# A float64-to-float32 weight conversion: the sign byte moves from VectorE to GpSimd, one buffer and a 32-byte pad are added

## The chip, the cores and the metric

One core of a Trainium2 chip runs the whole program. The metric is the device time of one execution in microseconds, the median of several runs. Engines are called PE (TensorE's matmuls), PEld (its weight loads), DVE (VectorE), ACT (ScalarE), POOL (GpSimd) and SP (SyncE, which only issues transfers here).

## What is computed

```python
attn = softmax(mask(q @ k.T / sqrt(64))) @ v          # 4 batches, 8 heads, 576 tokens, head size 64
x    = heads side by side                             # 2304 tokens x 512
x    = ((x @ w_a) * (x @ w_b)) @ w_out                # 512 -> 1536 -> 512
h    = x @ w_in;  out = (h * sigmoid(h)) @ w_out2     # 512 -> 2048 -> 512
```

Heads 0 to 3 see the last 32 keys, heads 4 to 7 every 32nd key. The weights come as float64, 8 bytes each; the activations are float32.

## The kernel before

**Stages.** The tokens are five groups of 512 (the last has 256). Attention of batch 0 stands ahead of all; the batches 1 to 3 are worked in between the first feed-forward work, by a plan. Then come 136 blocks for the groups 0 and 1: per block 12 matmuls of 128x512 with one weight piece of 128x512 (2.72 us of PE). Groups 2 and 3 follow together, by a scheme of seven products in place of eight (`Chain` from line 1005, `twin` from 1087): its products take sums of activations as moving operands, one after the other `A11, A12, S2, S1, S3, A22, S4`, in that order of `CHAIN_ORDER`, 12 matmuls each for a pair of chains (a "twin"). There are ten twins: six in the first feed-forward, four in the second, there with pieces of three other matmuls between halves of six. `A11`, `A12` and `S3` lie in tiles of `xpool`; `S2`, `S1`, `A22` and `S4` in the tile `operands` of the pool `late` (`open_late`). Group 4 comes partly between, partly last.

**Weights.** A float32 product is made of two rounded parts, so each weight piece is split: ACT writes the rounded part (L728), DVE the rest (L729, `split_w`), and the 12 matmuls of a block wait for both. Ahead of that, 68 pieces are converted from float64 once, by steps over the two 32-bit words of each number:
- `load_words` (L659, L661, on SP's queue) brings 512 KB into one of five buffers `words`, four blocks before the conversion (phase A).
- `rebase_w` (step B, L685, ACT) scales the high word into `e`.
- `merge_w` step 0 (L702, ACT) makes the three bits that come from the low word's top byte, as a whole 32-bit word of `raw`. Step 1 (L705, DVE) writes the sign bit over that word's top byte. Step 2 (L708, DVE) shifts `e` left and ors the word in.
- `keep_w` (L721) stores the piece to DRAM through POOL's queue, one block later, for the later token groups. `load_raw` (L675, SP) brings kept pieces back.

The first six pieces (`EARLY`) are converted during the attention of batch 0, where POOL does step 0 (L698); the other 62, which the change is about, in blocks 3 to 91. `raw` tiles take turns in the five buffers of `rpool`, `words` in the five of `kpool`.

**What sets the order.** Each engine runs its instructions in the order in which `block` writes them. That order is a string per phase:

```python
STEPS = ("NRM0BK1O2YXW", "N0O1B2MKWYRX")    # phase A, phase B
```

N is the softmax's guard, reciprocal and POOL product (L511, L518, L524), M its mask and maximum (L473, L484), X its exponentials (L499), O the store of attention results (L623, L626), R transposes of q and k (L288), K `keep_w`, Y `split_w`, W the loads. An instruction that waits holds back all that stand behind it on its engine.

**Memory.** Pools on the left are laid one after the other from below (`rpool`, then `wpool`, `spool`, `kpool`, `epool` behind it); `lpool`, `qpool`, `apool` are laid from the top downwards, and later `late` takes their place. In the built program every tile on the left but the narrow softmax ones starts at a multiple of 64 bytes within a partition, and the tile `operands` at byte 167904, which is 32 past one.

Of the kernel before, what the change touches and what calls it, by code (L numbers as in the profile page):

```python
# [9 lines left out]
F32 = mybir.dt.float32  # L10
F32R = mybir.dt.float32r
BF16 = mybir.dt.bfloat16
I32 = mybir.dt.int32
U8 = mybir.dt.uint8
AF = mybir.ActivationFunctionType
# [98 lines left out]
def attention_gated_mlp_silu_mlp(  # L114
# [35 lines left out]
    xpool = ctx.enter_context(tc.tile_pool(name="xpool", bufs=1))  # L150
    hpool = ctx.enter_context(tc.tile_pool(name="hpool", bufs=4))
    tpool = ctx.enter_context(tc.tile_pool(name="tpool", bufs=2))
    rpool = ctx.enter_context(tc.tile_pool(name="rpool", bufs=5))
    wpool = ctx.enter_context(tc.tile_pool(name="wpool", bufs=5))
    spool = ctx.enter_context(tc.tile_pool(name="spool", bufs=4))
    kpool = ctx.enter_context(tc.tile_pool(name="kpool", bufs=5))
# [3 lines left out]
    ringp = ctx.enter_context(tc.tile_pool(name="ringp", bufs=2, space=bass.MemoryType.PSUM))  # L160
    attp = ctx.enter_context(tc.tile_pool(name="attp", bufs=2, space=bass.MemoryType.PSUM))

    att_ctx = ExitStack()
    lpool = att_ctx.enter_context(tc.tile_pool(name="lpool", bufs=1, side="right"))
    qpool = att_ctx.enter_context(tc.tile_pool(name="qpool", bufs=2, side="right"))
# [520 lines left out]

    made = {}

    def merge_w(c, step, early=False):
        if c is None or (c < EARLY and not early):  # L690
            return
        high = words[c].bitcast(U8).rearrange("p (n eight) -> p n eight", eight=8)[:, :, 7]
        if step == 0:
            made[c] = rpool.tile([P, DM], F32, tag="raw", name="raw")
            z = made[c].bitcast(I32)
            top = words[c].bitcast(U8).rearrange("p (n eight) -> p n eight", eight=8)[:, :, 3]
            if early:
                nc.gpsimd.tensor_scalar(  # L698
                    out=z, in0=top, scalar1=1.0 / 32, scalar2=-31.0 / 64, op0=ALU.mult, op1=ALU.add
                )  # L700
            else:
                nc.scalar.activation(out=z, in_=top, func=AF.Copy, scale=1.0 / 32, bias=-31.0 / 64)  # L702
        elif step == 1:
            out = made[c].bitcast(U8).rearrange("p (n four) -> p n four", four=4)[:, :, 3]
            nc.vector.tensor_single_scalar(out=out, in_=high, scalar=SIGN, op=ALU.bitwise_and)  # L705
        else:
            z = made[c].bitcast(I32)
            nc.vector.scalar_tensor_tensor(  # L708
                out=z, in0=rebased.pop(c), scalar=3, in1=z, op0=ALU.logical_shift_left, op1=ALU.bitwise_or
            )  # L710
            del words[c]
            if c < NA:
                raw[c] = made[c]

    def keep_w(c):

        if c in made:
            kept[pieces[c]] = t = dpool.tile([P, DM], F32, tag="kept%s%d" % pieces[c], name="kept%s%d" % pieces[c])

            queue = nc.sync if c < EARLY else nc.gpsimd  # L720
            queue.dma_start(out=t, in_=made.pop(c))  # L721
# [74 lines left out]
    def block(p):  # L796


        background(p, "load")
        w = split.pop(p)  # L800
        yield w
        c = conv_at.get(p)
        for step in STEPS[p >= NA]:
            if step == "K":
                keep_w(conv_at.get(p - 1))
            elif step == "B":
                rebase_w(c)
            elif step in "012":
                merge_w(c, int(step))
            elif step == "Y":  # L810
                split_w(p + AHEAD_SPLIT)
            elif step == "W":
                load_words(conv_at.get(p + AHEAD_WORDS - AHEAD_MERGE))
                load_raw(p + (7 if p < last_conv + 2 else 9))
            else:
                background(p, {"M": "mask", "O": "store", "X": "softmax", "N": "normalise", "R": "prepare"}[step])
        background(p + 1, "tensor", "turned")
        yield None
# [680 lines left out]
```

## Time and profile before

| | us |
|---|---|
| three runs | 924.67, 928.13, 928.27 (median 928.13) |
| the profiled execution | 925.8 |
| its span, first to last instruction | 924.0 |
| PE, PEld busy | 901.9 (98%), 733.5 (79%) |
| DVE, ACT, POOL busy | 642.6 (70%), 533.3 (58%), 92.8 (10%) |
| mean granted clock of PE | 0.988 |

The profile gives each engine's busy time; a matmul's end is modelled, so one that starts late shows in the distance between starts rather than in its length. The blocks 0 to 135 lie in about 56 to 474 us of the span (the attention of batch 0 fills what is ahead), the twins of the first feed-forward in 474 to 614, those of the second in 706 to 823, group 4 between and behind them. Lines are those of the kernel before.

### The profile page before, as it was taken

The numbers are of one execution on the slowest core, as the hardware profiler recorded it, in microseconds if no ns is written. First come the engines' busy times: TensorE is split into PE (matmuls) and PEld (weight loads), VectorE is DVE, ScalarE is ACT, GpSimd is POOL, SyncE is SP. The second block draws the span as 40 slices with busy tenths as digits, with TensorE's granted clock in tenths as the row PEclk, the third lists the DMA queues.
The fourth block names the chain that finished last, engine by engine and source line by source line (L and its number), as shares of the span: only waits on it lengthen the run. The fifth ranks groups of instructions, "written<-read, shape, count | busy, mean of one in ns | idle before, by whom it ended". The sixth has DMA issues, their size and how long they took to land.

```text
span 924.0 us, 16415 instructions
## 1 busy us (share of the span) xinstructions
PE 901.9 (98%) x5907; PEld 733.5 (79%) x5914; DVE 642.6 (70%) x1215; ACT 533.3 (58%) x1270; POOL 92.8 (10%) x162
## 2 busy tenths in 40 slices
PE   8899899999999999999999999999999999999998
PEld 5577677787778878778888888888999878878897
DVE  3577888776767867666677676655687766766475
ACT  4657788665677665564544344355575655554474
POOL 4532222011111010100000000000000000000000
PEclk9699999999999999999999999999999999999999
DMA  9999899999799992323332112233463121225471
GB/s 163 191 295 252 291 267 277 274 245 271 220 261 257 290 279 87 126 80 96 104 112 76 53 55 66 68 103 103 136 183 115 47 91 57 81 81 170 123 205 39
DMA packets 163697, 145.32 MB, mean 157 GB/s; under 512 B 96848, under 2 KB 119952, under 8 KB 163616
## 3 DMA queue, kind: packets, MB, share of 16 engines
q1 hardware_dynamic: 154758, 121.81, 49.6%
q0 software_dynamic: 6912, 21.66, 7.1%
q10 hardware_dynamic: 1946, 0.81, 0.4%
q8 instruction: 46, 0.75, 0.3%
q14 instruction: 35, 0.29, 0.1%
HBM read 121.70 MB, written 22.54 MB: 156 GB/s over the span
## 4 chain that ended last, share of the span: by engine, by line
PE 71%; DVE 9%; ACT 7%; DMA 7%; issue 4%; SPq 2%; POOL 0%; DVEq 0%; ACTq 0%; POOLq 0%
PE ring L736 16%; PE ring L1022 12%; PE att L1022 9%; PE acc L1083 8%; PE acc L1437 6%; PE acc L1209 4%; PE ring L1083 4%; PE att L1083 4%; PE acc L736 3%; PE acc L1417 3%; ACT prs L499 2%; DVE w L729 2%; DMA words<-in_moe_w_b_dram 1%; DMA keptb<-raw 1%; DVE raw L708 1%
## 5 line engine op out<-in xcount | busy, mean ns | idle before, releaser
L736 PE MATMUL ring<-x,w 128*128 128x512 f32 (+1 forms) x816 | 166.4, 356 | 4.8 <-DVE w L729 3.3
L736 PEld LDWEIGHTS ring<-x,w 128*128 128x128 f32 x816 | 132.2, 189 | 30.7 <-DVE w L729 7.6
L1313 DVE TENSOR_TENSOR w<-raw,w 128x512 fp32r<-128x512 f32 (+1 forms) x164 | 106.2, 655 | 29.3 <-ACT w L1312 26.5
L1312 ACT CAST w<-raw 128x512 fp32r<-128x512 f32 (+1 forms) x164 | 95.7, 592 | 20.8 <-PE att L1083 11.0
L729 DVE TENSOR_TENSOR w<-raw,w 128x512 fp32r<-128x512 f32 x136 | 93.4, 693 | 4.9 <-ACT w L728 4.7
L1437 PE MATMUL acc<-w,h 128*128 128x512 f32 x384 | 93.7, 393 | 1.3 <-DVE w L729 0.9
L736 PE MATMUL ring<-y,w 128*128 128x512 f32 x384 | 93.6, 393 | 0.3 <-DVE w L729 0.3
L1437 PEld LDWEIGHTS acc<-w,h 128*128 128x128 f32 x384 | 71.3, 188 | 18.1 <-DVE w L729 2.1
L736 PEld LDWEIGHTS ring<-y,w 128*128 128x128 f32 x384 | 71.3, 188 | 15.9 <-DVE w L729 0.7
L728 ACT CAST w<-raw 128x512 fp32r<-128x512 f32 x136 | 82.5, 619 | 2.2 <-PE acc L736 1.3
L1417 PE MATMUL acc<-h,w 128*128 128x512 f32 x288 | 72.3, 397 | 3.6 <-DVE w L729 2.5
L746 ACT CAST h<-h 128x512 fp32r<-128x512 f32 (+1 forms) x48 | 27.2, 567 | 83.8 <-DVE h L1058 41.0
L1417 PEld LDWEIGHTS acc<-h,w 128*128 128x128 f32 x288 | 52.8, 188 | 17.8 <-DVE w L729 4.6
L1022 PE MATMUL ring<-operands,w 128*128 128x512 f32 x240 | 61.3, 398 | 0.0
L1022 PE MATMUL att<-operands,w 128*128 128x512 f32 x240 | 60.4, 396 | 0.0
L747 DVE TENSOR_TENSOR h<-g,h 128x512 fp32r<-128x512 f32 (+1 forms) x64 | 39.9, 624 | 28.9 <-ACT h L746 28.9
L1022 PE MATMUL ring<-x,w 128*128 128x512 f32 x240 | 59.4, 391 | 0.0
L746 ACT CAST h<-g 128x512 fp32r<-128x512 f32 (+1 forms) x64 | 36.3, 567 | 37.5 <-DVE g L1409 30.5
L1128 POOL DMA_DIRECT2D out_dram<-o x16 | 8.7, 545 | 467.4 <-DVE o L1127 467.0
L499 ACT ACTIVATE prs<-sm,nm 128x54 f32<-128x54 f32 (+1 forms) x120 | 39.8, 333 | 25.1 <-DVE nm L484 25.1
L1022 PEld LDWEIGHTS ring<-operands,w 128*128 128x128 f32 x240 | 44.9, 188 | 11.7 <-DVE w L1313 1.1
L1022 PEld LDWEIGHTS att<-operands,w 128*128 128x128 f32 x240 | 45.1, 188 | 10.9
(202 smaller groups left out, 1559.4 us busy)
## 6 DMA issues: line engine op xcount, KB each, us to landing
raw<-keptp SPq DMA_DIRECT2D x80, 256.0 KB
raw<-kepti SPq DMA_DIRECT2D x64, 256.0 KB
words<-in_moe_w_out_dram SPq DMA_DIRECT2D x28, 512.0 KB
raw<-kepto SPq DMA_DIRECT2D x48, 256.0 KB
raw<-kepta SPq DMA_DIRECT2D x36, 256.0 KB
raw<-keptb SPq DMA_DIRECT2D x36, 256.0 KB
words<-in_moe_w_in_dram SPq DMA_DIRECT2D x16, 512.0 KB
words<-in_moe_w_a_dram SPq DMA_DIRECT2D x12, 512.0 KB
```

The source lines that it names most:

```text
L499: nc.scalar.activation(out=place[s], in_=src[s], func=AF.Exp, bias=st["nm"][:, s:s + 1], scale=1.0, accum_out=su[:, s:s + 1],)
L728: nc.scalar.copy(out=o[:, 0], in_=t)
L729: nc.vector.tensor_tensor(out=o[:, 1], in0=t, in1=o[:, 0].bitcast(F32), op=ALU.subtract)
L736: nc.tensor.matmul(ps[:, :T], lhsT=w[:, wi, c * P:(c + 1) * P], rhs=x[:, xi, c, :T], start=(c == 0 and wi == 0 and xi == 0), stop=(c == CC ...
L746: nc.scalar.copy(out=o[:, 0, :T], in_=t32[:, :T])
L747: nc.vector.tensor_tensor(out=o[:, 1, :T], in0=t32[:, :T], in1=o[:, 0, :T].bitcast(F32), op=ALU.subtract)
L1022: nc.tensor.matmul(self.acc[acc], lhsT=w[:, wi, (2 * part + c) * P:(2 * part + c + 1) * P], rhs=x[:, xi, c], start=(begin and c == 0 and m ...
L1083: nc.tensor.matmul(accs[d], lhsT=lhsT, rhs=rhs, start=(first and wi == 0 and xi == 0), stop=(last and wi == 1))
L1312: nc.scalar.copy(out=o[:, 0, cols], in_=t)
L1313: nc.vector.tensor_tensor(out=o[:, 1, cols], in0=t, in1=o[:, 0, cols].bitcast(F32), op=ALU.subtract)
L1417: nc.tensor.matmul(accs[d], lhsT=w[:, wi, d * P:(d + 1) * P], rhs=h[:, xi], start=(j == 0 and wi == 0 and xi == 0), stop=(j == N1 - 1 and ...
L1437: nc.tensor.matmul(accs[t][:, :DM], lhsT=h[:, xi, t * P:(t + 1) * P], rhs=w[:, wi, :], start=(j == 0 and wi == 0 and xi == 0), stop=(j == ...
```

## The change

For the 62 later pieces the sign is made by POOL one block ahead: it allocates the `raw` tile and writes a whole word, -2^31 or 0 (`sign_w`, called at step 1 with the piece of block p+1). ACT's step 0 then writes only the lowest byte of each word of that tile. DVE's step 1 is gone for them; step 2 is as before. Since a tile is taken one block sooner, `rpool` has six buffers, which moves the pools behind it up by 2048 bytes; a pad of 32 bytes at the top of the right side moves all tiles there down by 32 bytes, `operands` to byte 167872, a multiple of 64. Other tiles move likewise: `qT`, `kT`, `vl`, `qld`, `kld` from 32 past a multiple of 64 onto one; `vs`, `prs`, `ptl`, `pt` and the masks from a multiple to 32 past one.

```diff
-    rpool = ctx.enter_context(tc.tile_pool(name="rpool", bufs=5))
+    rpool = ctx.enter_context(tc.tile_pool(name="rpool", bufs=6))
...
+    ppool = ctx.enter_context(tc.tile_pool(name="ppool", bufs=1, side="right"))
+    ppool.tile([P, 8], F32, name="pad")
...
+    def bytes_of(t, size, at):
+        return t.bitcast(U8).rearrange("p (n size) -> p n size", size=size)[:, :, at]
+
+    def sign_w(c):
+        if c is None or c < EARLY:
+            return
+        made[c] = rpool.tile([P, DM], F32, tag="raw", name="raw")
+        nc.gpsimd.tensor_scalar(
+            out=made[c].bitcast(I32), in0=bytes_of(words[c], 8, 7), scalar1=float(SIGN), scalar2=-(2.0 ** 31),
+            op0=ALU.is_ge, op1=ALU.mult,
+        )
...
             else:
-                nc.scalar.activation(out=z, in_=top, func=AF.Copy, scale=1.0 / 32, bias=-31.0 / 64)
+                nc.scalar.activation(
+                    out=bytes_of(made[c], 4, 0), in_=top, func=AF.Copy, scale=1.0 / 32, bias=-31.0 / 64
+                )
...
-            elif step in "012":
+            elif step in "02":
                 merge_w(c, int(step))
+            elif step == "1":
+                sign_w(conv_at.get(p + 1))
```

On POOL, in phase A during the attention of batch 1 (L721, now L738, stores a converted piece; L524, now L526, is the softmax's product; L700 is the new sign). Before:

```order
L524 TENSOR_TENSOR prs_111<-prs_111,rs 128x256
L721 DMA keptb_1469<-raw 128x512
L524 TENSOR_TENSOR prs_109<-prs_109,rs 128x256
L721 DMA kepto_1511<-raw 128x512
L524 TENSOR_TENSOR prs_110<-prs_110,rs 128x128
```

Now:

```order
L526 TENSOR_TENSOR prs_115<-prs_115,rs 128x256
L738 DMA keptb_1474<-raw 128x512
L700 TENSOR_SCALAR raw<-words 128x512
L526 TENSOR_TENSOR prs_113<-prs_113,rs 128x256
L738 DMA kepto_1516<-raw 128x512
L700 TENSOR_SCALAR raw<-words 128x512
L526 TENSOR_TENSOR prs_114<-prs_114,rs 128x128
```

The sign for block p+1 stands behind the softmax product of block p and the store of the piece of block p-1, and ahead of the softmax product of block p+1.

On DVE at the same place (L705 the sign byte, L708 the merge, now L725; L729 the split, now L746). Before:

```order
L288 STREAM_TRANSPOSE kT<-kld 128x18x32
L705 TENSOR_SCALAR raw<-words 128x512
L708 SCALAR_TENSOR_TENSOR raw<-e,raw 128x512
L729 TENSOR_TENSOR w<-raw,w 128x512
L288 STREAM_TRANSPOSE kT<-kld 128x18x32
L705 TENSOR_SCALAR raw<-words 128x512
L708 SCALAR_TENSOR_TENSOR raw<-e,raw 128x512
L729 TENSOR_TENSOR w<-raw,w 128x512
```

Now:

```order
L290 STREAM_TRANSPOSE kT<-kld 128x18x32
L725 SCALAR_TENSOR_TENSOR raw<-e,raw 128x512
L746 TENSOR_TENSOR w<-raw,w 128x512
L290 STREAM_TRANSPOSE kT<-kld 128x18x32
L725 SCALAR_TENSOR_TENSOR raw<-e,raw 128x512
L746 TENSOR_TENSOR w<-raw,w 128x512
```

The sign's row is gone and nothing else has changed places; ACT has the same rows in the same order.

## Rows read from the trace of the kernel before

**Rows 1.** Busy time by stretch: us, then busy us of PE, PEld, DVE, ACT, POOL
```profile
56.00:130.00 74.00, 69.70 (x604) 53.28 (x603) 59.91 (x121) 54.47 (x144) 16.91 (x29) 1.00 0.98 270
130.00:345.00 215.00, 210.67 (x1656) 167.74 (x1655) 159.16 (x302) 150.50 (x381) 33.41 (x59) 1.00 1.00 264
...
474.00:656.00 182.00, 182.00 (x794) 148.70 (x793) 119.01 (x206) 80.58 (x149) 2.20 (x4) 1.00 0.26 80
...
706.00:833.00 127.00, 126.74 (x552) 102.05 (x551) 90.81 (x162) 69.43 (x132) 0.00 (x0) 1.00 0.24 73
```

**Rows 2.** Timeline of PE, 97 to 112 us; in brackets the idle time before
```profile
99.18 2.56 PE L736 MATMUL ring<-x,w 128*128 128x512 f32 x10 [1.24 <-DVE w L729]
...
111.30 0.97 PE L736 MATMUL ring<-x,w 128*128 128x512 f32 x3 [1.21 <-DVE w L729]
```

**Rows 3.** Timeline of DVE, 108 to 112 us
```profile
108.30 1.25 DVE L288 STREAM_TRANSPOSE kT<-kld 128x576 f32<-128x576 f32 x1
109.39 0.45 DVE L705 TENSOR_SCALAR raw<-words 128x512 uint8<-128x512 uint8 x1
...
111.16 1.25 DVE L288 STREAM_TRANSPOSE kT<-kld 128x576 f32<-128x576 f32 x1
```

**Rows 4.** Chain that ended last, pieces in order: start us, us, what
```profile
84.18 7.20 DMA words<-in_moe_w_b_dram
...
101.23 0.46 DVE raw L705
...
318.77 0.40 DVE raw L705
```

**Rows 5.** Groups by line: count, busy us, mean ns, idle time before them
```profile
L728 ACT CAST w<-raw 128x512 fp32r<-128x512 f32 x136 | 82.5, 619 | 2.2 <-PE acc L736 1.3 <-DVE raw L708 0.9
...
L702 ACT ACTIVATE raw<-words 128x512 int32<-128x512 uint8 x62 | 41.5, 670 | 10.0 <-DMA words<-in_moe_w_a_dram 2.0 <-DMA kepto<-raw 2.0 <-issue 1.7
...
L705 DVE TENSOR_SCALAR raw<-words 128x512 uint8<-128x512 uint8 x68 | 32.1, 472 | 16.3 <-ACT raw L702 12.0 <-POOL raw L698 3.9
```

**Rows 6.** Timeline of POOL, two stretches
```profile
24.29 0.65 POOL L698 TENSOR_SCALAR raw<-words 128x512 int32<-128x512 uint8 x1
...
131.30 0.92 POOL L524 TENSOR_TENSOR prs<-prs,rs 128x324 f32<-128x324 f32 x1 [2.33 <-ACT raw L702]
132.17 0.57 POOL L721 DMA_DIRECT2D kepto<-raw  x1
```

**Rows 7.** Timeline of DVE, 131 to 135 us
```profile
131.78 0.99 DVE L708 SCALAR_TENSOR_TENSOR raw<-e,raw 128x512 int32<-128x512 int32 x1
...
133.98 0.69 DVE L708 SCALAR_TENSOR_TENSOR raw<-e,raw 128x512 int32<-128x512 int32 x1
```

**Rows 8.** Timeline of ACT, 132 to 134 us
```profile
132.62 0.67 ACT L702 ACTIVATE raw<-words 128x512 int32<-128x512 uint8 x1
```

**Rows 9.** Chain that ended last, first feed-forward's twins: start us, us, what
```profile
476.65 2.72 PE att L1022 x12
479.37 2.81 PE ring L1022 x12
482.18 2.80 PE att L1022 x12
...
493.36 2.76 PE ring L1022 x12
```

**Rows 10.** Timeline of PE in the second feed-forward's twins
```profile
755.26 0.86 PE L1083 MATMUL acc<-w,h 128*128 128x512 f32 x3
755.96 1.56 PE L1022 MATMUL ring<-operands,w 128*128 128x512 f32 x6
757.36 0.86 PE L1083 MATMUL acc<-w,h 128*128 128x512 f32 x3
```

**Rows 11.** Chain that ended last, two pieces of attention matmuls: start us, us, what
```profile
213.85 1.31 PE att L458 x80
...
237.56 1.30 PE att L593 x80
```

More of the change, by code (lines that the diff above doesn't have):

```diff
@@ L691, in merge_w @@
             return
-        high = words[c].bitcast(U8).rearrange("p (n eight) -> p n eight", eight=8)[:, :, 7]
         if step == 0:
-            made[c] = rpool.tile([P, DM], F32, tag="raw", name="raw")
-            z = made[c].bitcast(I32)
-            top = words[c].bitcast(U8).rearrange("p (n eight) -> p n eight", eight=8)[:, :, 3]
+            top = bytes_of(words[c], 8, 3)
             if early:
+                made[c] = rpool.tile([P, DM], F32, tag="raw", name="raw")
                 nc.gpsimd.tensor_scalar(
-                    out=z, in0=top, scalar1=1.0 / 32, scalar2=-31.0 / 64, op0=ALU.mult, op1=ALU.add
+                    out=made[c].bitcast(I32), in0=top, scalar1=1.0 / 32, scalar2=-31.0 / 64, op0=ALU.mult, op1=ALU.add
                 )
             else:
-                nc.scalar.activation(out=z, in_=top, func=AF.Copy, scale=1.0 / 32, bias=-31.0 / 64)
+                nc.scalar.activation(
+                    out=bytes_of(made[c], 4, 0), in_=top, func=AF.Copy, scale=1.0 / 32, bias=-31.0 / 64
+                )
         elif step == 1:
-            out = made[c].bitcast(U8).rearrange("p (n four) -> p n four", four=4)[:, :, 3]
-            nc.vector.tensor_single_scalar(out=out, in_=high, scalar=SIGN, op=ALU.bitwise_and)
+            nc.vector.tensor_single_scalar(
+                out=bytes_of(made[c], 4, 3), in_=bytes_of(words[c], 8, 7), scalar=SIGN, op=ALU.bitwise_and
+            )
         else:
@@ L715, in keep_w @@
     def keep_w(c):
-        if c in made:
+        if c is not None and c in made:
             kept[pieces[c]] = t = dpool.tile([P, DM], F32, tag="kept%s%d" % pieces[c], name="kept%s%d" % pieces[c])
```

## The prediction

> **What bounds the kernel now.** I read the busy time by stretch first. In the twins of both feed-forwards PE is busy without a gap: 182.00 of 182 us and 126.74 of 127 [rows 1]. DVE and ACT have room there, so whatever shortens a matmul shortens the kernel, and nothing else does. In 56 to 345 us, where the 62 pieces are converted, PE is idle for 74 - 69.70 = 4.3 us and 215 - 210.67 = 4.3 us [rows 1], 8.6 us together. That is small, but DVE is busy 60 of 74 us in the first of these stretches, and what ends PE's gaps is the split on DVE: two of them, 1.24 and 1.21 us, lie within 13 us [rows 2]. The DVE rows of that place tell why: from one transpose of k to the next, one block apart, 111.16 - 108.30 = 2.86 us pass [rows 3], and DVE hardly stops in them, while PE needs 2.72 us for a block. The sign byte is 0.45 us of these 2.86 [rows 3]. So there DVE sets the pace by a little, and the byte is more than the difference. The chain that ended last says the same over the whole stretch: it runs through L705 in 12 pieces, the first 0.46 and the last 0.40 us long, 4.8 us in all (both ends of that list are in [rows 4]).
>
> **The change, part by part.**
>
> *The sign byte leaves DVE.* 62 instructions of 472 ns [rows 5] are 29 us of DVE's time. Only what lies on the path counts: 4.8 us by the chain. It can be less than that, since behind a shorter DVE stands ACT, whose cast has to end before the split; it can't be much more than PE's 8.6 us of idle time. I take 4.8.
>
> *ACT's step 0 writes a byte of each word in place of a word.* The trace has no ACT instruction with a byte out at that step. The nearest rows: 670 ns for L702 as it is, 619 ns for the plain cast L728 [rows 5]; and L705, which writes bytes four apart on another engine, isn't slow at 472. I take no change. The bounds are 0.05 us less and, by the same distance upwards, 0.05 us more; the chain has 18 pieces of L702, so plus or minus 0.9 us.
>
> *The sign on POOL.* The instruction nearest to it reads one byte in eight of `words` and writes 512 words: 0.65 us undisturbed [rows 6]. 62 of them are 40 us on an engine that is busy 17 + 33 of 289 us [rows 1], so POOL has the time. What it delays is the store behind it and the next softmax product, by 0.65 us each; nobody waits for either at that distance. I count this at nothing; the cover is POOL's idle time, and where POOL waits, ACT is late next:
>
> *ACT now waits for POOL.* The sign is queued behind the store of the piece two before it, which waits for that piece's L708, and behind a softmax product. Mostly there are over 1 us to spare before ACT's step 0. I set each L702's start against the end of the POOL row that would stand in front of its sign, plus 0.7 us: it comes out late in 3 of 62 places, 1.7 us in all. The worst: the store in front ends at 132.17 + 0.57 = 132.74 [rows 6], so the sign would end at 133.4, and ACT began at 132.62 [rows 8]. I take 0.5 us of these 1.7 for the path.
>
> *Late words.* In 75 to 99 us the chain is the loading of words, for instance 7.20 us from 84.18 [rows 4], and L702 begins at once when they have landed. There the sign now stands between landing and ACT, 0.65 + 0.1 us, in at most three of the chain's pieces: 0 to 2.2 us, and I take 1.0, since the pieces that follow are set by transfers and not by ACT. Against it: a `words` buffer is now let go by ACT and POOL, no longer by L705, which can bring loads forward where DVE is late. I count that at nothing, because after 99 us the words mostly have time in hand.
>
> *DVE and POOL together.* L708 takes 0.99 us where it begins inside a softmax product of POOL and 0.69 us two instructions later, where it doesn't [rows 7]; the POOL product took 0.92 us [rows 6]. So a hit costs DVE about 0.3 us. The Trainium skill (SBUF — State Buffer, Who interferes with whom) states the rule: a VectorE instruction with two SBUF inputs contends with a GpSimd instruction that reads SBUF, and the later one is blocked until the other is done. By that rule alone L708, begun 0.44 us before the product's end, would have taken 1.13 us; the 0.99 is on its side, if a little less. How often will a sign be hit? It starts behind a store that itself begins after L708, 0.3 + 0.57 us later, when the split L729 (0.69 us) is nearly done; the DVE rows that follow are then often reads from PSUM or waits. I take one sign in twenty on the path: 3 x 0.3 = 1 us. The lower end is nothing, the upper end is a rival below.
>
> *Six raw buffers.* The tile is taken a block sooner and there is one more, so the distance to the store that must have landed is the same. Nothing in either direction; later loads of kept pieces have one buffer more, in a stretch where PE doesn't wait.
>
> *The pad.* The twins' rows show a pattern that repeats in all ten: 12 matmuls with `A12` take 2.72 us; the next group, with `S2`, takes 2.81, the one with `S1` 2.80; the first aligned group after such ones takes 2.76 [rows 9]. The slow ones are the four operands in the tile `operands`, 32 bytes past a multiple of 64; the fast ones lie on one. `A22` and `S4` repeat it. A twin thus holds 0.09 + 0.08 + 0.04 + 0.09 + 0.08 + 0.04 = 0.42 us over 2.72 a group, six twins 2.5 us. In the second feed-forward a half group takes 757.36 - 755.96 = 1.40 us where half of 2.72 is 1.36, and the three matmuls ahead of it 0.70 where a quarter is 0.68 [rows 10]: 8 x 0.04 + 8 x 0.02 = 0.48 us a twin, four twins 1.9 us. If the place in memory is the cause, 4.4 us go, all of them on the path, as PE has no gap there. That it is the place is inferred: matmuls of equal shape, equal weights' pool and equal result banks differ by nothing else that I see. The bounds are 0 and 4.4; I take 4.4 because every one of the ten twins shows it and no group with another operand does.
>
> *Tiles that lose their multiple of 64.* `ptl` and `pt`, which L593 reads, are now 32 off, and `kT`, which L458 reads, was 32 off before. 80 of the one take 1.30 us and 80 of the other 1.31 [rows 11]. The two will change places, and I count nothing; at most a tenth of some 12 us either way.
>
> **The sum**, against the profiled execution: 925.8 - 4.8 + 0.5 + 1.0 + 1.0 - 4.4 = 919.1 us. That execution was 2.3 us below the median of the runs shown (928.13), within their spread of 924.67 to 928.27; a median has to lie between 919.1 and 921.4. I forecast **919.5 us**.
>
> **The rivals.**
>
> 1. *The conversion gives nothing, the pad does.* ACT paces the bursts as much as DVE, so the freed 0.47 us turn into waits for `rebase_w`. For it: ACT is busy 150.50 of 215 us there, near DVE's 159.16 [rows 1]. Against it: the gaps in rows 2 end with DVE. 925.8 - 4.4 = 921.4, up to 923.7 on the median. Chance 0.20.
> 2. *The pad gives nothing, the conversion does.* The slow groups would then come from something else that the tile `operands` has, its place far from `x` for instance. 925.8 - 2.3 = 923.5 to 925.8. Chance 0.10.
> 3. *Both give all.* PE's 8.6 us of idle time in 56 to 345 us vanish: 925.8 - 8.6 - 4.4 = 912.8. Against it: some of that time is loading, not DVE. Chance 0.13.
> 4. *POOL blocks DVE, and the kernel is slower.* Place: L708, L729 and L747, each with two inputs in SBUF; the chain has 21 + 23 + 7 = 51 pieces of them in 56 to 345 us. If each is hit at 0.30 us [rows 7], that is 15.3 us: 925.8 + 15.3 - 4.8 - 4.4 = 931.9. It decides from (4.8 + 4.4) / 0.30 = 31 hits on the path. For it: half the softmax products of POOL were hit. Against it: those are issued when DVE is in the middle of a conversion, the sign is issued after one. Chance 0.06. By the skill's rule with the whole 0.65 us of a sign each time, the same case would be 51 x 0.65 = 33 us, near 950; no row shows such a hit.
>
> The forecast itself has 0.51. A measurement of this kernel can tell about 0.5% (4.6 us) from no change, so faster means under 923.5. The forecast and rival 3 lie there, 0.64, and about half of rival 1 and a fifth of rival 2, 0.12: 0.76 faster. Of the rest 0.18 are the same (the other parts of rivals 1 and 2, a little of rival 4) and 0.06 slower. The range takes in rival 3 and the upper ends of 1 and 2: 912.5 to 925.5.
>
> **What would show it.** In the changed kernel's profile every group of 12 matmuls in the twins takes 2.72 us, and L1022's groups agree whatever their operand: the pad is right. If they still alternate, it is not. DVE's busy time falls by about 29 us to some 614, POOL's rises by 40 or more; PE's gaps before 345 us that end with the split are shorter or fewer, and their sum falls by 2 to 5 us. L702's successor stays at about 0.67 us. Wrong would be: L708 or L729 longer on average by over 0.1 us (rival 4), ACT's step 0 waiting for POOL by more than 3 us in all, or ACT's byte write above 0.72 us.

## The result and the profile after

| | us, median | range | ratio to before, 95% |
|---|---|---|---|
| before | 924.67 | 924.06 to 928.27 | |
| changed | 931.84 | 930.98 to 932.02 | 1.0069 [1.0055, 1.0083] |

Two more runs of the kernel before than stand ahead of the prediction make its median 924.67, no longer 928.13. By the ratio the kernel became 0.69% slower, 6.4 us; the medians are 7.2 us apart, and the ratio is what is used below. The prediction said 919.5, within 912.5 to 925.5: faster, where the kernel became slower. The profiled execution of the changed kernel has a span of 930.1 us, against 924.0 before.

Busy time by stretch of the changed kernel, the columns as in [rows 1]:

```profile
56.00:130.00 74.00, 68.68 (x597) 52.20 (x596) 53.95 (x99) 53.38 (x133) 56.65 (x49) 1.00 0.95 266
130.00:345.00 215.00, 205.50 (x1550) 162.00 (x1549) 144.15 (x253) 150.78 (x376) 120.87 (x101) 1.00 0.93 253
...
474.00:656.00 182.00, 182.00 (x799) 149.52 (x797) 124.33 (x218) 81.53 (x151) 2.20 (x4) 1.00 0.25 80
```

In the two stretches of the conversion PE is idle for 5.3 + 9.5 = 14.8 us, where it was 8.6 [rows 1]. DVE did become freer, by 6 and 15 us, as the change wants it. But POOL, the last busy column, went from 16.91 + 33.41 to 56.65 + 120.87 us: 127 us more, where the prediction counted with 40. The groups by line say which row that is (L700 is the sign; L716, L725 and L746 answer to L702, L708 and L729 of [rows 5]):

```profile
L700 POOL TENSOR_SCALAR raw<-words 128x512 int32<-128x512 uint8 x62 | 129.0, 2081 | 42.1 <-DMA words<-in_moe_w_out_dram 13.2 <-DMA words<-in_moe_w_in_dram 12.5 <-DVE w L746 4.6
...
L716 ACT ACTIVATE raw<-words 128x512 uint8<-128x512 uint8 x62 | 49.1, 792 | 18.6 <-POOL raw L700 18.6
L746 DVE TENSOR_TENSOR w<-raw,w 128x512 fp32r<-128x512 f32 x136 | 99.4, 737 | 4.4 <-ACT w L745 4.2
L725 DVE SCALAR_TENSOR_TENSOR raw<-e,raw 128x512 int32<-128x512 int32 x68 | 52.9, 778 | 44.6 <-ACT e L687 25.5 <-issue 14.5 <-DMA words<-in_moe_w_b_dram 2.0
```

Four things differ from what was assumed. The sign takes 2081 ns on average and not 650. ScalarE's step 0 takes 792 ns and not 670, and it has waited 18.6 us for POOL. VectorE's two rows with two inputs in SBUF are 44 and 61 ns longer on average than before (693 and 717). And POOL has come onto the path: the chain that ended last runs through L700 for 11.3% of 56 to 345 us. Some rows of POOL, DVE, PE and ACT from 130 to 139 us show how these hang together; in brackets is the idle time before a row:

```profile
130.50 1.96 POOL L700 TENSOR_SCALAR raw<-words 128x512 int32<-128x512 uint8 x1
130.50 1.20 DVE L746 TENSOR_TENSOR w<-raw,w 128x512 fp32r<-128x512 f32 x1
...
131.76 2.56 PE L753 MATMUL ring<-x,w 128*128 128x512 f32 x10 [1.13 <-DVE w L746]
...
134.20 2.48 POOL L700 TENSOR_SCALAR raw<-words 128x512 int32<-128x512 uint8 x1
...
134.80 1.11 DVE L746 TENSOR_TENSOR w<-raw,w 128x512 fp32r<-128x512 f32 x1
...
135.97 2.57 PE L1436 MATMUL acc<-h,w 128*128 128x512 f32 x10 [0.89 <-DVE w L746]
...
136.72 0.80 ACT L716 ACTIVATE raw<-words 128x512 uint8<-128x512 uint8 x1 [1.93 <-POOL raw L700]
137.26 1.97 POOL L700 TENSOR_SCALAR raw<-words 128x512 int32<-128x512 uint8 x1
...
138.10 0.69 DVE L725 SCALAR_TENSOR_TENSOR raw<-e,raw 128x512 int32<-128x512 int32 x1 [2.18 <-issue]
```

The sign of 134.20 ends at 136.68; ScalarE has stood 1.93 us for it, and VectorE's merge behind ScalarE 2.18 us. The two splits at 130.50 and 134.80 took 1.20 and 1.11 us beside a sign, where one without POOL beside it takes 0.68, and PE stood still until they had ended, 1.13 and 0.89 us. The merge at 138.10 lies wholly inside a sign and took 0.69, as without one: being beside POOL isn't always being hit.

The pad did something, but not what was forecast. The chain that ended last in the twins of the first feed-forward, start us, us, what:

```profile
484.04 2.72 PE att L1041 x12
486.76 2.76 PE ring L1041 x12
489.53 2.75 PE att L1041 x12
492.27 5.53 PE ring L1041 x24
```

These answer to 2.72, 2.81, 2.80 and 2.76 in [rows 9], 7.4 us later than there. The groups on `operands` are shorter, yet not 2.72; the 24 in the last row are an aligned group that still takes 2.77 and the next on `operands`.

### The profile page after: what moved, and what is told of

Same layout as the page of the kernel before. It is cut to its first block, busy times and chain, and to the rows that moved or that the text cites. A ratio compares the mean times of both kernels' runs of the same rounds, so it can differ in the third digit from the quotient of the medians.

```text
span 930.1 us, 16288 instructions
## 1 busy us (share of the span) xinstructions
PE 904.6 (97%) x5914; PEld 733.1 (79%) x5914; DVE 627.7 (67%) x1153; ACT 537.6 (58%) x1270; POOL 220.6 (24%) x224
## 4 chain that ended last, share of the span: by engine, by line
PE 70%; ACT 8%; DVE 7%; POOL 5%; issue 5%; DMA 3%; SPq 2%; POOLq 0%; DVEq 0%; ACTq 0%
PE ring L753 15%; PE ring L1041 12%; PE att L1041 9%; PE acc L1102 8%; PE acc L1456 6%; PE acc L1228 4%; PE att L1102 4%; PE ring L1102 4%; POOL raw L700 4%; PE acc L753 2%; PE acc L1436 2%; ACT prs L501 2%; ACT raw L716 2%; DVE raw L725 1%; DMA vs<-in_v_dram 1%
## 5 line engine op out<-in xcount | busy, mean ns | idle before, releaser
L700 POOL TENSOR_SCALAR raw<-words 128x512 int32<-128x512 uint8 x62 | 129.0, 2081 | 42.1 <-DMA words<-in_moe_w_out_dram 13.2
L746 DVE TENSOR_TENSOR w<-raw,w 128x512 fp32r<-128x512 f32 x136 | 99.4, 737 | 4.4 <-ACT w L745 4.2
L1456 PEld LDWEIGHTS acc<-w,h 128*128 128x128 f32 x384 | 71.3, 188 | 17.9 <-DVE w L746 2.0
L725 DVE SCALAR_TENSOR_TENSOR raw<-e,raw 128x512 int32<-128x512 int32 x68 | 52.9, 778 | 44.6 <-ACT e L687 25.5
L716 ACT ACTIVATE raw<-words 128x512 uint8<-128x512 uint8 x62 | 49.1, 792 | 18.6 <-POOL raw L700 18.6
```

Source lines behind the costliest of these rows:

```text
L700: nc.gpsimd.tensor_scalar(out=made[c].bitcast(I32), in0=bytes_of(words[c], 8, 7), scalar1=float(SIGN), scalar2=-(2.0 ** 31), op0=ALU.is_ge ...
L716: nc.scalar.activation(out=bytes_of(made[c], 4, 0), in_=top, func=AF.Copy, scale=1.0 / 32, bias=-31.0 / 64)
L746: nc.vector.tensor_tensor(out=o[:, 1], in0=t, in1=o[:, 0].bitcast(F32), op=ALU.subtract)
L1456: nc.tensor.matmul(accs[t][:, :DM], lhsT=h[:, xi, t * P:(t + 1) * P], rhs=w[:, wi, :], start=(j == 0 and wi == 0 and xi == 0), stop=(j == ...
```

## The experiments

Four theories stood at the start. **T1a**: the long sign makes ScalarE late. **T2**: ScalarE's byte write costs. **T3**: POOL's reading slows VectorE's rows with two inputs in SBUF. **T4**: what the pad gives depends on another multiple than 64. There were 14 runs, of 13 kernels, each against the kernel before on the same chip (medians of before 924.8 to 925.7). Differences between two of them are given in us as the difference of their ratios times 925; with intervals of about 0.001 each way, such a difference is good to some 1.5 us.

### The pad

**pad32** is the kernel before with the pad of the change alone; **pad96** the same with three times the pad:

```diff
+    ppool = ctx.enter_context(tc.tile_pool(name="ppool", bufs=1, side="right"))
+    ppool.tile([P, 8], F32, name="pad")     # pad96: [P, 24]
     att_ctx = ExitStack()
```

> The kernel before with the 32-byte pad alone. Theory of the prediction: the pad is worth 4.4 us, so about 920.3 against 924.7 for the kernel before on the same chip (ratio 0.995), groups on operands at 2.72 us. Theory formed from the changed kernel's trace: the groups go only to 2.764 and 2.746, 0.24 us of excess left in a twin of 0.42, so 1.5 to 2 us: about 923.0 (0.998). A third: the pad gives nothing and those shorter groups came from the changed conversion, 924.7.

> The kernel before with a pad of 96 bytes in place of 32. The pad of 32 put operands at 167872, a multiple of 64 and not of 128; the operands that run at 2.72 us (x, h) and the weights all begin at multiples of 128. With 96 bytes operands begins at 167808, a multiple of 128. Theory 'the place modulo 128 decides': all groups 2.72 us, the 4.4 us come in full, about 920.3 (ratio 0.995). Rival 'the place modulo 64 decides, and the rest of the excess is something else, the distance from x for instance': as with 32 bytes, groups 2.764 and 2.746, about 923.0 (0.998).

Measured: pad32 922.78 us, ratio 0.9975 [0.9965, 0.9985], so 2.3 us; pad96 916.77 us, 0.9909 [0.9896, 0.9922], so 8.4 us. From the first matmul on `operands` to the last, the trace has 343.9 us in the kernel before, 342.5 with 32 bytes and 340.1 with 96. The same chain with 96 bytes:

```profile
475.67 2.72 PE att L1024 x12
478.39 5.44 PE ring L1024 x24
483.83 2.72 PE att L1024 x12
486.55 2.72 PE ring L1024 x12
```

Every group takes 2.72 us. So the place in memory is the cause, and the multiple is 128: `operands` lay at 167904 before (96 past a multiple of 128), at 167872 in the change (64 past one), at 167808 here, which is a multiple of 128 and not of 256. But 8.4 is more than the twins' 3.8. Two kernels part the gain. **late96** moves `operands` alone, **att96** all but `operands`:

```diff
# late96
             t = pool.tile([P, 16, G], F32R, name="operands")
+            pool.tile([P, 24], F32, name="pad")
# att96
     att_ctx = ExitStack()
+    ppool = att_ctx.enter_context(tc.tile_pool(name="ppool", bufs=1, side="right"))
+    ppool.tile([P, 24], F32, name="pad")
```

> The kernel before with 96 bytes put in behind the tile operands alone, so that it begins at 167808, a multiple of 128; nothing else in memory moves, q, k, v and the attention's tiles lie as before. The stretch of the twins took 343.9 us in the kernel before, 342.4 with the 32-byte pad and 340.1 with 96 bytes; the rest of the 8.7 us that the 96 bytes gave lies ahead of them, most of it in the first 56 us. Theory 'two gains, one from operands in the twins and one from the attention's tiles at the start': 925 - 3.8 = 921 (ratio 0.996). Rival 'the start differs by chance, or by something that operands sets': as with 96 bytes for all, 917 (0.991).

> The kernel before with a pad of 96 bytes that is given back before the tile operands is placed: the attention's tiles of q, k and v begin at multiples of 128, operands lies 32 bytes past a multiple of 64 as before. With 96 bytes for all the kernel took 916.8, with 96 bytes at operands alone 920.1, against 925.3 before. Theory 'two gains that add': 925.3 - (8.7 - 4.3) = about 921 (ratio 0.995), the twins' stretch 343.9 us as before, the first split done about 3 us sooner than at 33.1 us. Rival 'the start of that run was luck': 924 to 925.5 (ratio 0.999 or more).

Measured: late96 920.13, 0.9954 [0.9942, 0.9966], 4.3 us; att96 921.30, 0.9959 [0.9946, 0.9972], 3.8 us; together 8.1, near the 8.4 of pad96. They are two gains that add. For the second one the start was looked at. The first 56 us of the kernel before, of late96, att96 and pad96, one row from each; the last three columns are the granted clock, the DMA share and GB/s:

```profile
0.00:56.00 56.00, 48.10 (x623) 32.51 (x631) 28.75 (x92) 28.38 (x130) 28.43 (x52) 0.82 0.97 204
```
```profile
0.00:56.00 56.00, 47.91 (x632) 32.22 (x640) 30.27 (x95) 29.18 (x131) 29.39 (x53) 0.91 0.98 206
```
```profile
0.00:56.00 56.00, 49.14 (x646) 32.25 (x646) 31.09 (x97) 29.30 (x131) 29.17 (x53) 0.94 0.94 216
```
```profile
0.00:56.00 56.00, 48.70 (x703) 33.13 (x710) 32.21 (x99) 29.85 (x133) 30.51 (x55) 0.94 0.96 223
```

The DMA share is near 1 in all of them, and with the attention's tiles at multiples of 128 more bytes pass. The packet records say which: the 18432 packets of 128 bytes in the first 60 us (the rows of q and k) take 13.6 to 13.7 ns each on average in all five runs with those tiles at multiples of 128, and 15.6 to 17.9 ns in the eleven others (before 16.3). (16.3 - 13.7) x 18432 / 16 engines = 3.0 us, an estimate near the 3.8. That the quicker packets are what shortens the kernel is argued from this and not shown by itself.

The granted clock of that stretch differs between these rows too: in the kernel before TensorE was granted the lower of its two levels, 1.2 in place of 2.4 GHz, for 20.5 us of it, in pad96 for 6.8. But it doesn't part the kernels: fused96 (below), with its tiles at multiples of 128, had 17.1 us of it and 13.7 ns a packet, and zero (below), without, 6.8 us and 15.7 ns. Nor is it worth 3.8 us: of the 72 runs of the kernel before, the 17 with a mean clock of 0.990 or less took 925.5 us on average, the 8 with 0.995 or more 924.7.

Two more runs asked whether the remaining attention tiles matter, which the change moved from 0 to 32 past a multiple of 64, and whether pad96 repeats:

```diff
# all128: pad96 and
+    gpool = att_ctx.enter_context(tc.tile_pool(name="gpool", bufs=1, side="right"))
+    gpool.tile([P, 24], F32, name="gap")
     apool = att_ctx.enter_context(tc.tile_pool(name="apool", bufs=3, side="right"))
```

> The kernel before with 96 bytes as in the run with 96 bytes for all, and 96 more between the tiles of q, k and the rest of the attention's tiles (qs, prs, ptl, pt, vs), so that these too begin at multiples of 128; so far they lay 64 past one (before), 32 or 96 (with the pads). The prediction counted nothing for them. Theory 'those tiles don't matter': as with 96 bytes for all, 917 (ratio 0.991), the two within 1 us of each other. Rival 'each operand and each load target off 128 costs': 2 to 4 us less, 913 to 915 (0.987 to 0.989); its size is estimated from the twins, where operands off 128 cost 1 to 3 per cent of a matmul, and from the loads of q and k, whose 128-byte packets took 13.7 ns at multiples of 128 and 16.3 ns in the kernel before.

> The kernel before with the pad of 96 bytes, once more, for comparison on the same chip: 917 (ratio 0.991). If it comes out at 920 or more, the part of its gain that lay at the start was chance.

Measured: all128 0.9919 [0.9903, 0.9934], pad96b 0.9924 [0.9909, 0.9940]. They agree, so `qs`, `prs`, `ptl`, `pt` and `vs` matter by no more than the 1.5 us that can be told, and the gain of pad96 isn't chance.

### The sign

**forms** prices six instructions in one kernel (each comment stands for one call):

```diff
+        if m == 0:    # is_ge 128, mult -2**31, as in the change
+        elif m == 1:  # mult 1/128, add -63/128
+        elif m == 2:  # is_ge 128, mult 1.0
+        elif m == 3:  # mult 1/128
+        elif m == 4:  # is_ge 128
+        else:         # fp32 high word, mult 0.0, fp32 out
```

> The changed kernel in which the piece number modulo 6 chooses one of six instructions for the sign on GpSimd, to price each: (0) as in the change; (1) product and sum, byte in, int32 out, the form of L698 that took 0.65 us; (2) compare and product with 1; (3) one product, byte in, int32 out; (4) the compare alone; (5) fp32 high word times 0.0. Except in (0) and (5) the weights' sign is lost. Theory 'the compare is slow': (0), (2) and (4) near 2.0 us, the others 0.6 to 0.8. Theory 'the large number into int32 is slow': (0) alone is near 2.0. Theory 'the place is slow, beside VectorE's work': all six near 2.0. Theory 'a second operation is slow': (0), (1), (2) longer than (3), (4), (5), against which stands L698 with 0.65 us for two.

The groups by line of that kernel, in the order of their cost; L703, L705, L707, L709, L711 and L713 are the six forms from 0 to 5:

```profile
L703 POOL TENSOR_SCALAR raw<-words 128x512 int32<-128x512 uint8 x11 | 22.4, 2038 | 8.1 <-DMA words<-in_moe_w_in_dram 4.3 <-DMA keptp<-raw 1.7 <-DMA words<-in_moe_w_b_dram 1.3
L707 POOL TENSOR_SCALAR raw<-words 128x512 int32<-128x512 uint8 x10 | 20.9, 2093 | 6.4 <-DMA words<-in_moe_w_in_dram 4.1 <-DMA words<-in_moe_w_a_dram 1.8
L711 POOL TENSOR_SCALAR raw<-words 128x512 int32<-128x512 uint8 x10 | 16.9, 1685 | 13.0 <-DMA words<-in_moe_w_in_dram 11.4 <-DMA words<-in_moe_w_out_dram 1.4
L713 POOL TENSOR_SCALAR raw<-words 128x512 f32<-128x512 f32 x10 | 16.5, 1651 | 5.7 <-DVE w L756 2.9 <-DMA words<-in_moe_w_out_dram 2.6
L709 POOL TENSOR_SCALAR raw<-words 128x512 int32<-128x512 uint8 x10 | 16.3, 1633 | 11.4 <-DMA words<-in_moe_w_out_dram 7.7 <-DVE w L756 2.1 <-DMA words<-in_moe_w_b_dram 1.4
...
L705 POOL TENSOR_SCALAR raw<-words 128x512 int32<-128x512 uint8 x11 | 9.1, 827 | 9.2 <-DMA words<-in_moe_w_out_dram 8.7
```

None of the four theories holds as it was put. One operation takes 1.63 to 1.69 us, compare or product, byte or fp32 alike; a compare and a product take 2.04 to 2.09; a product and a sum take 0.83, half of a product alone. The row that the prediction took its price from, L698 with 0.65 [rows 6], is of that one quick pair. It was the same engine, the same tiles and the same sizes, but not the same operations.

**zero** and **fused** put two of these into the change. The word times 0.0 keeps its sign as plus or minus zero, and a sum with -0.0 keeps that:

```diff
-            out=made[c].bitcast(I32), in0=bytes_of(words[c], 8, 7), scalar1=float(SIGN), scalar2=-(2.0 ** 31),
-            op0=ALU.is_ge, op1=ALU.mult,
+# zero:  tensor_single_scalar(out=made[c], in_=high.bitcast(F32), scalar=0.0, op=ALU.mult)
+# fused: tensor_scalar(out=made[c], in0=high.bitcast(F32), scalar1=0.0, scalar2=-0.0, op0=ALU.mult, op1=ALU.add)
```

> The changed kernel with another instruction for the sign on GpSimd: the high word, read as fp32, times 0.0, which leaves plus or minus zero, one operation with fp32 in and out in place of a compare and a product with a byte in and int32 out. All else as in the change. Theory T1 (the sign's 2.08 us on GpSimd is what costs: ScalarE's step 0 waits for it, VectorE runs slower beside it): if the new one takes 0.6 to 0.8 us, the wait of ScalarE for GpSimd falls from 18.6 us to under 4, and the time comes down from 931.8 by 6 to 11 us, to 921 to 926. Theory T2 (ScalarE's byte write, 0.79 in place of 0.67 us, 7.6 us in all, is what costs): the time falls by 3 us at most, to 929 or more, though GpSimd is short. If the new instruction too takes about 2 us, the form isn't the cause of its length and the time stays at 931 to 932.

> The changed kernel with the high word as fp32 times 0.0 plus -0.0 for the sign, a product and a sum in one instruction; the six forms showed 0.83 us for a product and a sum, 1.65 for a product alone. Theory T1 (the length of the sign on GpSimd costs the time, by ScalarE's wait and the rows beside it): the sign takes 0.65 to 0.9 us, ScalarE waits for it under 3 us in all, and the kernel takes 919 to 922 us (ratio to before 0.994 to 0.997), under the kernel with the 32-byte pad alone (922.8). Theory T2 (ScalarE's byte write sets the end): 924 or more, with no wait of ScalarE for GpSimd left. If the sum with -0.0 isn't of the quick kind: as with the product alone, 927.

Measured: zero 927.43, 1.0023 [1.0014, 1.0032], with 1646 ns a sign and 11.6 us of ScalarE's waiting; fused 924.44, 0.9995 [0.9985, 1.0005]:

```profile
L701 POOL TENSOR_SCALAR raw<-words 128x512 f32<-128x512 f32 x62 | 46.1, 744 | 63.3 <-DMA words<-in_moe_w_out_dram 22.7 <-DMA words<-in_moe_w_in_dram 16.6 <-DMA words<-in_moe_w_b_dram 5.0
...
L716 ACT ACTIVATE raw<-words 128x512 uint8<-128x512 uint8 x62 | 49.1, 792 | 6.3 <-POOL raw L701 6.3
L746 DVE TENSOR_TENSOR w<-raw,w 128x512 fp32r<-128x512 f32 x136 | 100.0, 741 | 3.9 <-ACT w L745 3.5
L725 DVE SCALAR_TENSOR_TENSOR raw<-e,raw 128x512 int32<-128x512 int32 x68 | 51.8, 762 | 35.0 <-ACT e L687 18.1 <-issue 11.0 <-POOL raw L701 2.6
```

The quick sign takes back 6.8 us of the change, but fused doesn't come under pad32 (0.9975): I had expected 919 to 922 and missed. ScalarE's waiting is down to a third, and the split and the merge are as long as with the slow sign. That pointed to T3.

**nosign**, **dummy**, **dummyfast** and **ahead2** take the change apart, all with the 32-byte pad:

```diff
# nosign: pad32, without L705 for the 62 pieces
# dummy:  nosign and, at the change's place (high: byte 7 of each eight of words[c]),
+    jpool = ctx.enter_context(tc.tile_pool(name="jpool", bufs=2))
+        nc.gpsimd.tensor_scalar(out=jpool.tile([P, DM], I32, tag="scrap", name="scrap"), in0=high,
+            scalar1=float(SIGN), scalar2=-(2.0 ** 31), op0=ALU.is_ge, op1=ALU.mult)
# dummyfast: dummy with the product and sum of fused
# ahead2: the change with
-    rpool = ctx.enter_context(tc.tile_pool(name="rpool", bufs=6))
+    rpool = ctx.enter_context(tc.tile_pool(name="rpool", bufs=7))
-                sign_w(conv_at.get(p + 1))
+                sign_w(conv_at.get(p + 2))
```

> The kernel before with the 32-byte pad and without L705 for the 62 late pieces: no engine makes their sign, so all these weights are taken as positive; ScalarE writes whole words as before. It prices the first term of the prediction alone, VectorE rid of the byte. By that term (4.8 us on the chain): 922.8 - 4.8 = 918.0 (ratio 0.992). Rival 'ScalarE sets the pace as much': 922 to 923 (0.9975). Rival 'VectorE sets all of the idle time of PE in that stretch': 914 (0.988).

> As the kernel without a sign, but GpSimd makes the changed kernel's sign (compare and product, 2.08 us) at the changed kernel's place, into a tile of its own that nobody reads; ScalarE writes whole words and waits for no GpSimd. The sign is lost here too. It takes the wait of ScalarE and its byte write away and leaves GpSimd's load beside VectorE. Theory T1a (the wait of ScalarE costs most): near the kernel without a sign, 0 to 3 us above it. Theory T3 (GpSimd's long reads slow VectorE's two-input rows, and that costs most): 6 to 10 us above it, with the split's and the merge's mean longer by 0.04 us or more.

> As the run with GpSimd's sign into a tile that nobody reads, but with the quick instruction (product and sum in fp32, 0.74 us in place of 2.08). ScalarE writes whole words and waits for no GpSimd; the sign is lost. Over the kernel without a sign (916.9) there is only GpSimd's traffic beside VectorE. In the traces the excess of VectorE's two-input rows is some 11 to 14 us with the long and with the quick instruction alike. Theory 'each sign costs VectorE about the same whatever its length': 922 to 924.5, as with the long one (924.5). Theory 'the cost goes with GpSimd's busy time': a third of 7.6 us, about 919.5; then the rest of the 924.4 of the quick version is ScalarE's byte and wait.

> The changed kernel with the sign made two blocks ahead in place of one and seven raw buffers in place of six; the long instruction, ScalarE's byte write and the 32-byte pad as in the change. ScalarE should no longer wait for GpSimd (18.6 us in the changed kernel). Between the run with the sign into a tile nobody reads (924.5) and the changed kernel (931.8) lie the wait and the byte write. Theory T1a (the wait): 924.5 to 926.5 (ratio about 1.000). Theory T2 (the byte write, 62 times 0.12 us): 929 to 932 with the wait under 4 us.

| | ratio, 95% | what it adds to the line above | us |
|---|---|---|---|
| pad32 | 0.9975 [0.9965, 0.9985] | the pad | -2.3 |
| nosign | 0.9921 [0.9907, 0.9935] | VectorE rid of the byte | -5.0 |
| dummy | 0.9999 [0.9987, 1.0011] | POOL's slow sign beside it | +7.2 |
| ahead2 | 1.0002 [0.9991, 1.0012] | ScalarE's byte write, the sign used | +0.3 |
| the change | 1.0069 [1.0055, 1.0083] | ScalarE's wait for the sign | +6.2 |
| dummyfast | 0.9964 [0.9952, 0.9976] | over nosign: the quick sign beside it | +4.0 |

So T1a is shown with 6.2 us. POOL's sign beside the other engines costs 7.2; of these, 4.0 come with the quick sign too, which lengthens VectorE's rows as much. That is T3, shown by the traces below, though small delays behind the sign are in it. T2 isn't shown: the byte write is longer by 0.12 us, but 62 of them move the end by 0.3 us, less than such a difference is good for. Ahead2 has one `raw` buffer more than the change, as the earlier sign needs it; no run parts the two. The lines of nosign, of dummy and of ahead2:

```profile
L732 DVE TENSOR_TENSOR w<-raw,w 128x512 fp32r<-128x512 f32 x136 | 94.0, 696 | 6.1 <-ACT w L731 5.3 <-DMA kld<-in_k_dram 0.4
...
L711 DVE SCALAR_TENSOR_TENSOR raw<-e,raw 128x512 int32<-128x512 int32 x68 | 47.1, 693 | 32.7 <-ACT e L687 32.2
```
```profile
L695 POOL TENSOR_SCALAR scrap<-words 128x512 int32<-128x512 uint8 x62 | 131.7, 2125 | 40.2 <-DMA words<-in_moe_w_in_dram 18.8 <-DMA words<-in_moe_w_out_dram 17.9 <-DMA words<-in_moe_w_b_dram 1.2
...
L742 DVE TENSOR_TENSOR w<-raw,w 128x512 fp32r<-128x512 f32 x136 | 102.4, 759 | 5.3 <-ACT w L741 4.9
L721 DVE SCALAR_TENSOR_TENSOR raw<-e,raw 128x512 int32<-128x512 int32 x68 | 52.1, 767 | 33.4 <-ACT e L688 32.9
```
```profile
L716 ACT ACTIVATE raw<-words 128x512 uint8<-128x512 uint8 x62 | 49.1, 792 | 4.4 <-POOL raw L700 4.2
```

From nosign to dummy nothing of VectorE's own work changes, yet its split goes from 696 to 759 ns and its merge from 693 to 767: 136 x 0.063 + 68 x 0.074 = 13.6 us of VectorE's time. In ahead2 ScalarE's wait falls from 18.6 to 4.2 us.

VectorE's rows with one input in PSUM (`h<-ring,a`) are a control: in the changed kernel the 12 that began inside a sign took 681 ns on average, the 5 beside no POOL work 686. And for the rows with both inputs in SBUF the averages hide an exact pattern, which a sign of zero and one of fused show:

```profile
79.65 1.52 POOL L701 TENSOR_SCALAR raw<-words 128x512 f32<-128x512 f32 x1 [0.65 <-DMA words<-in_moe_w_out_dram]
79.85 0.98 DVE L723 SCALAR_TENSOR_TENSOR raw<-e,raw 128x512 int32<-128x512 int32 x1 [2.79 <-issue]
80.75 0.68 DVE L744 TENSOR_TENSOR w<-raw,w 128x512 fp32r<-128x512 f32 x1
```
```profile
85.49 0.66 POOL L701 TENSOR_SCALAR raw<-words 128x512 f32<-128x512 f32 x1 [1.67 <-DMA words<-in_moe_w_a_dram]
85.80 0.90 DVE L725 SCALAR_TENSOR_TENSOR raw<-e,raw 128x512 int32<-128x512 int32 x1
```

Taken at the 0.69 us of an undisturbed one, the merge at 79.85 was held until 80.14, 0.49 us after the sign's start, and the split at 80.75 inside the same sign not at all; the merge at 85.80 was held until 86.01, 0.52 after the start. The whole traces agree: rows that began inside a sign were held until 0.13 to 0.15 us before its end in fused (13 of 18 rows), 1.01 to 1.02 in zero (16 of 55), 1.44 to 1.45 in the changed kernel (15 of 70), and the others, but for one in the changed kernel, began near or after that point and were held by 0.04 us at most. Dummy and dummyfast agree with this but for one row each, ahead2 but for three. A sign alone takes 0.66, 1.53 and 1.95 us there, so it is each time its first 0.5 us that holds VectorE. That fits a sign of 0.7 us costing VectorE as much as one of 2. The rows shown above fit it too: the splits at 130.50 and 134.80 were held until 131.01 and 135.23, 1.45 us before the end of their signs (the second of these began inside a merge and is itself 0.53 us longer than one alone), and the merge at 138.10 began 0.84 us after its sign's start.

Dummyfast came out just under what its first theory expected (its 922 is a ratio of 0.9966) and far above the second. VectorE's split and merge have nearly the same means there (755 and 773 ns) as in dummy, but the end is 3.2 us earlier. What the 1.35 us of a longer sign delay besides would be a reason, and the traces have such delays: in 56 to 345 us SP's loads waited 8.0 us for dummy's sign and 3.0 for the quick one. The chain that ended last in dummy has a store queued behind a sign, and ScalarE's step 0, which needs the buffer that is stored, behind that:

```profile
217.74 1.90 POOL scrap L695
219.64 6.43 DMA keptp<-raw
226.09 0.66 ACT raw L714
```

ScalarE has waited 2.48 us there. No run takes these delays apart, so how the 3.2 us are made up stays open.

**fused96** joins the quick sign and 96 bytes (the edits of fused and of pad96).

> The changed kernel with both things mended that the runs have shown: the quick instruction for the sign on GpSimd and 96 bytes in place of 32. If the gains add: 924.4 - (922.8 - 916.8) = 918.4 (ratio 0.993), still above the kernel before with the pad of 96 bytes alone (916.8), so that the sign is better left with VectorE. If it comes out under 916, the pad and the sign help each other and the sign's move is worth having.

Measured: 919.02, 0.9937 [0.9920, 0.9954], as expected, and not better than the 96 bytes alone. The best version is pad96, 0.9909 and 0.9924 in two sets of runs, with all128 equal to it: the kernel before, with its sign on VectorE, and `operands` and the tiles of q and k at multiples of 128.

## Why the prediction was wrong

The sum was -4.8 + 0 + 0.5 + 1.0 + 1.0 - 4.4 = -6.7 us; measured was +6.4. Step by step:

- **The sign byte leaves DVE, -4.8.** Right: -5.0 by nosign against pad32. Reading the chain's pieces, not VectorE's 29 us of busy time, gave the size.
- **ACT's byte write, 0, within 0.9.** Its row was outside the bounds (0.79, not 0.62 to 0.72), its effect of 0.3 us inside.
- **The sign on POOL, 0.65 us, "I count this at nothing; the cover is POOL's idle time".** This is the step that failed, with what rested on it. The price came from L698, which fits in tile, size and engine and differs in its two operations. Measured: 2.08. POOL's idle time was not cover enough: the sign, the store and the softmax product are one queue, 2.08 + 0.59 of sign and store alone are nearly the 2.72 us of a block, and the chain runs through the sign for 11.3% of the stretch. Nor is it so that nobody waits for what stands behind the sign: in dummy ScalarE did, 2.48 us for one store.
- **ACT late behind POOL +0.5, late words +1.0.** Measured together: +6.2 (the change against ahead2, in which 4.2 us of waiting are left). The way of working it out, each ACT start against the end of the POOL row in front plus the sign, reaches half-way: with 2.08 in place of 0.7 it finds some 8 late places and about 9 us in the trace of before. The changed kernel has 17 waits, 18.6 us. The reckoning takes each sign alone and leaves out that a long sign delays the rows behind it and so the next sign; that this is the rest is argued.
- **DVE and POOL together, +1.0.** Measured: +7.2 with the slow sign, delays behind it included, +4.0 with the quick one. Even at the price that I assumed, this term was too small, because I let only one sign in twenty hit. In the changed kernel 44 of 62 merges and 51 of 85 splits between 56 and 345 us lie beside a sign; those that began inside a sign took 755 and 758 ns on average, those into which one began 950 and 985, and the ones beside no POOL work 689 and 684. That is 29 x 0.066 + 15 x 0.261 + 41 x 0.074 + 10 x 0.301 = 11.9 us. In fused it is 11.4, with fewer rows beside a sign that cost more each.
- **The pad, -4.4.** Its cause was right and its multiple wrong. 32 bytes bring `operands` to a multiple of 64 and gave 2.3 us, 1.4 of them in the twins; late96, at a multiple of 128, gave 4.3. The tiles that ran at 2.72 us, x and h, all lie at multiples of 128 too. I had asked what the slow and the fast tiles differ in and stopped at the first multiple that parts them.

Rival 4, POOL blocks DVE, gave 931.9 and had a chance of 0.06. Its number was met by luck, its account only half: it had 15.3 us of hits and the pad's 4.4, where 7.2 and 2.3 were measured, and no late ScalarE. Of the three signs that the text named for being wrong, two came: the wait above 3 us and the byte write above 0.72.

The rule that the prediction drew on (the Trainium skill, SBUF — State Buffer, Who interferes with whom) agrees with these traces in what collides: VectorE's rows with two inputs in SBUF, beside a POOL instruction that reads SBUF. Its further part, that the later one is held until the other is done, holds here for only the first 0.5 us of a sign: a merge or split that began in these was held until they were over, one that began later was not, however long the sign went on. So the 0.65 us a hit that the prediction reckoned by this rule, near 950, did not come.

## What to carry to other kernels

A price from a near row holds only for the same operations: on GpSimd the pair of ALU operations alone made 0.74 or 2.08 us of one size, and an engine that takes work over needs its queue added up per block, not its idle share. Work moved to GpSimd is paid by VectorE beside it, about 0.2 us of VectorE's time on average for each such instruction here whether it was quick or slow, where VectorE's rows have both inputs in SBUF; an order in which these begin over 0.5 us after GpSimd's should cost less, which no run here tried. Place operands of matmuls, and the targets of loads in 128-byte rows, at multiples of 128 bytes; here 96 bytes of nothing were worth more than the move of the sign could have been.

## What the runs showed of the hardware

- GpSimd's tensor-scalar on 128x512: a product and a sum 0.65 us undisturbed (L698 [rows 6]) and 0.74 to 0.83 on average in the blocks, one product or one compare 1.63 to 1.69, a compare and a product 2.04 to 2.13. A single product took 1.63 with bytes in and 1.65 with fp32. The Trainium skill (GPSIMD Engine Reference, Elementwise — side-by-side cycle accounting) gives 769 ns as measured for 512 elements in the best loop; the quick pair is near that, and undisturbed below it, the others are far beyond it.
- Such an instruction, quick or slow, holds a VectorE row with both inputs in SBUF through its first 0.5 us and no longer (fused, zero, the change); a row with one input in PSUM is not held.
- A matmul of 128x512 takes 227 ns from start to start where its moving operand begins at a multiple of 128 bytes; 12 of them took 2.75 to 2.76 us at 64 past one and 2.80 to 2.81 at 96 past one (32 past a multiple of 64), and the aligned group behind them was still up to 0.05 us longer.
- Loads in packets of 128 bytes took 13.6 to 13.7 ns a packet on average into tiles at multiples of 128 and 15.6 to 17.9 elsewhere.
- ScalarE needs 0.79 us to write every fourth byte where it writes whole words in 0.67, with the same input; it takes as long beside a slow sign as beside a quick one (792 ns in the change, in fused and in ahead2).
